# Attention and gated MLP on one core: q and k laid six tokens to a partition, later units cast by the Pool queue in order of use, tile 0 with gates ahead of values

## Chip, cores, metric

One of the cores of a Trainium2 chip runs the whole program. The metric is the device time of one execution in microseconds (us), the median of several runs. The span of a profile is some 1.7 us shorter than the time of the same execution, and moments within a run are counted from the span's start.

## The reference, cut to what matters

```python
def _attn_ref(q, k, v):                      # (8, 8, 576, 64) each, randn * 0.1
    scores = scale * np.matmul(q, k.transpose(0, 1, 3, 2))
    rel = pos[:, None] - pos[None, :]
    mask = (rel >= 0) & (rel < 64)           # causal, sliding window of 64
    scores = np.where(mask, scores, -1e9)
    attn = exp(scores - max); attn /= sum
    return attn @ v
def _moe_ref(x, w_gate, w_val, w_out):       # x: 4608 x 512, d_ff 1536
    return (np.maximum(x @ w_gate, 0) * (x @ w_val)) @ w_out
```

The inputs have a standard deviation of 0.1, so a score has one of about 0.01 (0.125 x 8 x 0.01) and the softmax is almost uniform in its window. A kernel that mixes up which token's q and k are which passes the comparison all the same.

## The kernel before

The sequence is worked in 24 units of 192 tokens (three per batch row); two units make a tile of 384 tokens. A unit's attention goes: load q and k, cast to FP16, transpose on VectorE (128x384 at a time), scores (`st`) on TensorE, exponential on ScalarE, values and row sums (`pv`) on TensorE, sums transposed, inverted and spread back on VectorE, and the normalised product (`xt`). A tile's MLP is 24 groups of four matmuls (`h`: 12 gate, 12 value groups) and 36 output matmuls (`op`). A small planner gives every step a wished time and so fixes the order of each engine's instructions; the engines then wait for data only.

```python
def qk_load(b, blocks=None, names="kq", two=False):      # a whole batch row (three units)
    ...
    eng = nc.gpsimd if b >= 2 else nc.scalar if two and g >= G // 2 else nc.sync
    eng.dma_start(nat[rows]...,                          # two tokens (512 B) to a run
        src[b, 2 * g:2 * g + 2].rearrange("h (m i j) d -> i (h m) (j d)", i=32, j=2))

def u_cast(u, name):                                     # rows 0 and 1 arrive as FP32
    if u < 3 and (u, name) not in ((0, "k"), (2, "k")):
        nc.scalar.copy(c16, src)
    else:
        nc.gpsimd.tensor_copy(c16, src)

def hidden(t, c0, c1, f0=0, f1=NF):                      # gate f, value f, gate f+1, ...
    for f in range(f0, f1):
        for i, wt in enumerate((wg, wv)):
            ...four matmuls into a bank of f_ps (4 banks)
...
    hidden(0, 0, U, 0, 4); ready(2); hidden(0, U, TT, 0, 4); hidden(0, 0, TT, 4)
    ready(3); hidden(1, 0, U)
    output_by_rows(0)
    ready(4); hidden(1, U, TT); output(1)
    for t in range(2, NU // 2):                          # the steady part
        ready(2 * t + 2); hidden(t, 0, TT); output(t)
```

"Second half of tile 0" below is `hidden(0, U, TT, ...)`: the first matmuls that need unit 1's `xt`. `heat` are matmuls on zeros that fill TensorE's idle time, meant to keep its clock up: the first four gate matmuls took 0.49 us in the changed kernel with eleven of them just before, and 0.80 without (e6).

The softmax here doesn't subtract the row's maximum and nothing guards it: scores larger than these inputs give would overflow.

## Time and profile before

| | us |
|---|---|
| time, median of 3 runs | 351.24 (350.97 to 351.8) |
| first gate matmul | 19.19 |
| second half of tile 0 starts | 25.65 |
| third tile (first of the steady part) starts | 82.48 (82.64 in the chain of waits, which the prediction uses) |
| each steady tile | 26.72 |
| tail | 27.16 |

Unit 1's `xt` is ready at 23.73, and the second half of tile 0 starts at 25.65 without a wait, behind the first half, which took 6.5 us:

```profile
7.13 3.44 POOL L192 DMA_DIRECT2D v<-in_v_dram  x4
...
22.77 0.96 DVE L343 TENSOR_TENSOR xt<-xv,rs 128x768 f16<-128x768 f32 x1 [0.37 <-ACT xv L318]
...
25.65 0.49 PE L398 MATMUL h<-xt,wg 128*128 128x192 f16 x4
```

### The profile page before, as it was taken

To read this page: it belongs to the slowest core of one execution; us is meant where nothing else is said; L and a number is where in the kernel's file an instruction comes from. 1 tells how busy PE (TensorE), PEld (TensorE's weight loads), DVE (VectorE), ACT (ScalarE), POOL (GpSimd) and SP (SyncE) were. 2 spreads that over 40 slices of the span, in tenths; PEclk is the share of its full clock that TensorE was granted. 3 is DMA by queue.
4 is the path that set the end of the run, shared out by engine and by line. 5 is a ranking of instruction groups with operands and counts; after the bars stand their busy time and mean duration, and the time that the engine had idled before them with its cause. 6 is when DMAs were issued, how large, how long until landed. Compare 5 with 4: busy or idle time off the path is not lost.

```text
span 350.3 us, 7421 instructions
## 1 busy us (share of the span) xinstructions
PE 334.8 (96%) x2910; PEld 200.6 (57%) x2910; DVE 232.9 (66%) x432; ACT 180.4 (52%) x346; POOL 89.2 (25%) x129
## 2 busy tenths in 40 slices
PE   8579989999999999999999999999999999999995
PEld 3467674865555655655665664664664664664652
DVE  6487756697766766766766766766776777675430
ACT  2745552746565464465564564563663663663331
POOL 5944022835110710134120720216110100000000
PEclk9859999999999999999999999999999999999999
DMA  6999999999833992429615894409906501001002
GB/s 189 165 204 191 213 196 95 186 94 189 91 25 99 90 97 92 32 18 184 81 11 112 63 111 107 30 3 158 121 2 104 49 2 60 33 0 62 30 2 90
DMA packets 95508, 32.21 MB, mean 92 GB/s; under 512 B 76017, under 2 KB 90865, under 8 KB 95473
## 3 DMA queue, kind: packets, MB, share of 16 engines
q0 software_dynamic: 80048, 17.57, 57.5%
q1 hardware_dynamic: 13760, 13.38, 13.3%
q10 hardware_dynamic: 1664, 0.79, 0.8%
q8 instruction: 23, 0.38, 0.4%
q14 instruction: 13, 0.10, 0.1%
HBM read 39.85 MB, written 9.44 MB: 141 GB/s over the span
## 4 chain that ended last, share of the span: by engine, by line
PE 70%; DMA 13%; DVE 8%; issue 4%; POOL 3%; SPq 1%; ACT 0%; DVEq 0%; POOLq 0%
PE h L398 37%; PE op L412 24%; PE pv L303 5%; DMA kn<-in_k_dram 5%; DVE g_sb L388 5%; DMA wv<-in_moe_w_val_dram 4%; DMA qn<-in_q_dram 4%; PE st L256 3%; DVE sT L329 3%; SPq L176 1%; POOL v L192 1%; DVE rT L335 1%; POOL wg L140 1%; POOL k L203 0%; POOL wv L140 0%
## 5 line engine op out<-in xcount | busy, mean ns | idle before, releaser
L398 PE MATMUL h<-xt,wv 128*128 128x384 f16 (+1 forms) x640 | 121.4, 313 | 2.7 <-DVE g_sb L388 1.4
L398 PE MATMUL h<-xt,wg 128*128 128x384 f16 (+1 forms) x640 | 121.3, 313 | 2.7 <-DVE xt L343 1.1
L388 DVE TENSOR_TENSOR g_sb<-r_sb,h 128x384 f16<-128x384 f32 (+1 forms) x160 | 79.6, 508 | 63.8 <-PE h L398 54.0
L385 ACT ACTIVATE r_sb<-h 128x384 f32<-128x384 f32 (+1 forms) x160 | 72.8, 464 | 57.9 <-PE h L398 43.3
L412 PE MATMUL op<-wo,g_sb 128*128 128x512 f16 x432 | 95.8, 379 | 0.5 <-DVE g_sb L388 0.3
L398 PEld LDWEIGHTS <-wg 128*128 128x128 f16 x640 | 60.7, 99 | 38.7 <-issue 4.7
L398 PEld LDWEIGHTS <-wv 128*128 128x128 f16 x640 | 60.5, 99 | 35.5 <-DMA wv<-in_moe_w_val_dram 2.1
L192 POOL DMA_DIRECT2D v<-in_v_dram x48 | 40.7, 851 | 156.4 <-PE pv L303 153.7
L412 PEld LDWEIGHTS <-g_sb 128*128 128x128 f16 x432 | 42.2, 98 | 49.9 <-issue 1.1
L329 DVE STREAM_TRANSPOSE sT<-pv 64x768 f32<-64x768 f32 x46 | 45.1, 980 | 23.4 <-ACT xv L318 20.3
L268 ACT ACTIVATE p<-st 128x512 f16<-128x512 f32 x96 | 53.0, 609 | 11.1 <-PE st L256 10.3
L419 ACT COPY o_sb<-op 128x512 f32<-128x512 f32 x36 | 20.9, 587 | 64.9 <-PE op L412 64.9
L318 ACT COPY xv<-pv 64x768 f32<-64x768 f32 x46 | 36.5, 793 | 25.9 <-PE pv L303 13.6
L272 DVE TENSOR_TENSOR p<-p,mask 128x512 f16<-128x512 f16 x88 | 33.7, 421 | 5.9 <-ACT p L268 5.7
L303 PE MATMUL pv<-p,v 128*128 128x128 f16 x368 | 25.4, 223 | 1.9 <-ACT p L268 1.9
L303 PEld LDWEIGHTS <-v 128*128 128x128 f16 x368 | 23.3, 100 | 5.1 <-DMA v<-in_v_dram 2.0
L337 DVE STREAM_TRANSPOSE rs<-rT 128x768 f32<-128x768 f32 x24 | 23.5, 978 | 0.8
L343 DVE TENSOR_TENSOR xt<-xv,rs 128x768 f16<-128x768 f32 x23 | 21.8, 949 | 0.8 <-ACT xv L318 0.4
L256 PE MATMUL st<-qT,kT 32*128 32x128 f16 x768 | 15.5, 215 | 1.6 <-DVE qT L216 1.2
L256 PEld LDWEIGHTS <-kT 32*128 32x128 f16 x768 | 11.3, 92 | 9.0 <-issue 7.6
L170 POOL DMA_DIRECT2D kh<-in_k_dram x24 | 15.8, 672 | 0.0
L170 POOL DMA_DIRECT2D qh<-in_q_dram x24 | 15.8, 679 | 0.0
(48 smaller groups left out, 80.7 us busy)
## 6 DMA issues: line engine op xcount, KB each, us to landing
out_dram<-o_sb SPq DMA_DIRECT2D x36, 256.0 KB, 2.0
v<-in_v_dram POOLq DMA_DIRECT2D x40, 128.0 KB, 4.1
kh<-in_k_dram POOLq DMA_DIRECT2D x24, 144.0 KB, 5.4
qh<-in_q_dram POOLq DMA_DIRECT2D x24, 144.0 KB, 7.1
wo<-in_moe_w_out_dram POOLq DMA_DIRECT2D x3, 512.0 KB, 15.9
kn<-in_k_dram SPq DMA_DIRECT2D x12, 96.0 KB, 7.1
qn<-in_q_dram SPq DMA_DIRECT2D x12, 96.0 KB, 5.9
wg<-in_moe_w_gate_dram POOLq DMA_DIRECT2D x2, 512.0 KB, 13.3
```

The costliest lines, as they stand in the source:

```text
L170: eng.dma_start(nat[rows].rearrange("p h m e -> p (h m) e"), src[b, 2 * g:2 * g + 2].rearrange("h (m i j) d -> i (h m) (j d)", i=32, j=2))
L192: nc.gpsimd.dma_start(v16[p0:128, w, :, 0:64], v[b, :, k0 + p0:k0 + 128].rearrange("h p d -> p h d"))
L256: nc.tensor.matmul(d["st"][g][:, (2 * hh + w) * 128:(2 * hh + w + 1) * 128], kT[rows, hh, ks + 128 * w:ks + 128 * w + 128, dh], d["qT"][ro ...
L268: nc.scalar.activation(d["p"][g].rearrange("p h c -> p (h c)"), d["st"][g], ACT.Exp, scale=scale)
L272: nc.vector.tensor_tensor(p, p, mask.rearrange("p w c -> p (w c)")[:, None, :].to_broadcast([128, 2, 256]), MUL)
L303: nc.tensor.matmul(pv[:, g, e, 64 * w:64 * w + 128], v16[:, w, c0:c0 + 128], d["p"][g][:, e, 128 * w:128 * w + 128], start=(e == 0 and w = ...
L318: nc.scalar.copy(d["xs"][rows], d["pv"][rows, :, g, 0:U])
L329: nc.vector.transpose(to[64 * e:64 * e + 64], d["pv"][64 - 64 * e:128 - 64 * e, :, e, 0:U])
L385: nc.scalar.activation(r_sb[:, 0:n], h1[:, 0:n], ACT.Relu)
L388: nc.vector.tensor_tensor(g_sb[:, f, c0:c1], r_sb[:, 0:n], h2[:, 0:n], MUL)
L398: nc.tensor.matmul(h[:, 0:n], wt[:, c, f * 128:f * 128 + 128], xt[:, c, c0:c1], start=(c == 0), stop=(c == NC - 1))
L412: nc.tensor.matmul(op, g_sb[:, f, bass.ds(sub * 128, 128)], wo[:, f], start=(f == 0), stop=(f == NF - 1))
```

## The change

Its intent: longer runs from memory (six tokens, 1,536 B), half the bytes landed for units 2 to 5 (the Pool queue casts on the way: 48 KB a transfer, where units 0 and 1 land 96), every transfer issued in the order in which it is used, gates before values in tile 0, and finer PSUM buffers for scores and values. Units 0 and 1 still arrive as FP32; VectorE now casts unit 1 and half of unit 0.

```diff
-    a_ps = ... tc.tile_pool(name="a_ps", bufs=1, space=PSUM)
+    a_ps = ... tc.tile_pool(name="a_ps", bufs=2, space=PSUM)      # two tiles of half the size
+    def qk_load(u, names="kq", queues=None):                       # one unit
+            for g in (0, 2, 1, 3):
+                part = src[b, 2 * g:2 * g + 2, U * uu:U * uu + U].rearrange("h (i j) d -> i h (j d)", j=6)
+                (nc.gpsimd if direct else queues[g // 2]).dma_start(nat[32 * g:32 * g + 32], part)
...
+            (nc.vector.tensor_copy if h or u else nc.scalar.copy)(c16[:, h], d[name][:, h])      # u_cast
...
-        nc.vector.transpose(dst.rearrange("p h (m i j) -> p h m j i", i=32, j=2), src)
+        nc.vector.transpose(dst.rearrange("p h (i j) -> p h j i", j=6), src)
...
+        for fb in range(f0, f1, each):                             # `each` gates, then `each` values
...
+        qk_load(0, "k", (nc.sync, nc.scalar))
+        qk_load(0, "q", (nc.sync, nc.scalar))
+        qk_load(1, "kq", (nc.sync, nc.sync))
...
+        W.at(3.0, lambda: v_load(0))
+        W.at(3.1, lambda: v_load(1))
+        ...six weight chunks at 3.2, q, k, v of unit 2, three w_out chunks, units 3, 4, 5
+        W.at(6.1, lambda: u_bias(1))
+        W.at(9.5, lambda: heat(11))
+        plan_unit(1, 9.0, (6.3, 7.5), (-1.8, -0.6), 1.3, None, 4.3, ...)
...
+        hidden(0, 0, U, 0, 4, 4); ready(2); hidden(0, U, TT, 0, 4, 4); hidden(0, 0, TT, 4, NF, 4)
+        output_by_rows(0)
+        ready(3); hidden(1, 0, U); ready(4); hidden(1, U, TT); output(1)
```

## The prediction

> **What bounds the kernel now.** I read the stretches first, because a busy share over the whole span mixes stages. Columns of this view: stretch, its length, then busy time and instructions of PE, PEld, DVE, ACT and POOL, granted clock, DMA share (it can pass 1[...]), GB/s.
>
> ```profile
> 0.00:19.19 19.19, 12.90 (x142) 7.11 (x143) 11.03 (x26) 8.67 (x15) 12.89 (x26) 0.90 1.16 180
> 19.19:40.00 20.81, 18.91 (x168) 13.66 (x169) 16.27 (x30) 11.51 (x24) 7.88 (x12) 0.85 1.43 200
> 40.00:62.00 22.00, 19.80 (x214) 13.86 (x216) 13.18 (x28) 9.49 (x23) 6.61 (x9) 1.00 1.25 153
> 62.00:82.64 20.64, 19.76 (x213) 14.06 (x208) 17.07 (x35) 11.84 (x27) 14.24 (x21) 1.00 1.60 150
> 82.64:109.37 26.73, 26.68 (x231) 15.47 (x229) 18.98 (x35) 14.52 (x27) 4.58 (x6) 1.00 0.78 97
> ```
>
> From 82.64 us on, each tile of 384 tokens takes 26.72 us and TensorE works 26.67 of it: nothing but fewer matmuls can help there. There are nine such tiles and a tail of 27.16 us. So the time is 82.64 + 9 x 26.72 + 27.16, and the change can win only before 82.64.
>
> Before it, the first gate matmul starts at 19.19. From there the work is two tiles, 31.5 of hidden matmuls (0.65 per group of four, 0.33 per half) and 15.5 of output, and units 2 to 5 at 1.57 each (0.57 scores, 0.89 values, 0.11 refill): 53.3 us. It takes 63.45: **10.1 us are lost**, and 19.19 us go before. The timeline of TensorE says where (start, duration, what, idle time and releaser):
>
> ```profile
> 19.19 0.80 PE L398 MATMUL h<-xt,wg 128*128 128x192 f16 x4 [1.08 <-DVE xt L343]
> 20.81 0.82 PE L398 MATMUL h<-xt,wv 128*128 128x192 f16 x4 [0.82 <-DMA wv<-in_moe_w_val_dram]
> ...
> 36.36 0.82 PE L398 MATMUL h<-xt,wv 128*128 128x384 f16 x4 [0.49 <-DMA wv<-in_moe_w_val_dram]
> ...
> 48.57 0.49 PE L398 MATMUL h<-xt,wv 128*128 128x192 f16 x4 [1.37 <-DVE g_sb L388]
> ```
>
> The first eight groups take 6.5 us where 2.6 would do: part waits, part half clock (0.50 granted from 20 to 25). The 1.37 at 48.57 is not VectorE's own slowness: its timeline has a transpose there that waited 1.62 for a Pool cast, and Pool had waited 4.77 for q. The chain of waits confirms it:
>
> ```profile
> 14.21 14.51 DMA wv<-in_moe_w_val_dram
> ...
> 33.68 6.73 DMA kn<-in_k_dram
> 40.42 5.73 DMA qn<-in_q_dram
> 46.17 7.17 DMA kn<-in_k_dram
> ...
> 53.84 5.63 DMA qn<-in_q_dram
> ```
>
> Apart from Pool's issuing, the path to 60 us is transfers, and the DMA view of 0 to 60 shows the engines full from 2.5 to 57 us with 10.97 MB moved. The head is **DMA-bound**.
>
> [...]weights (1,024 B landed per packet) run at about 205 GB/s between 20 and 26 us, a lone v load (128 B) lands 0.26 MB in 2.3 us, 113 GB/s. [...]q and k on SP and weights on Pool together keep near 200 GB/s, not twice that. [...]Output stores land in 2.0 us here.[...]
>
> **The change part by part.**
>
> *Layout.* Six tokens to a partition make runs of 1,536 B instead of 512 B. Units 2 to 5 are cast on the way instead of landing as FP32: 3.15 MB become 1.57 MB, 7 us of engine time in the head. Their Pool and ScalarE casts (0.83 each) go.
>
> *Pool's price.* Eight issues per unit instead of eight per three units. v issues of 512 and 1,024 runs took 0.69 and 0.88, so about 0.50 plus 0.37 ns per run; 64 runs should take 0.52. That is 4.2 us per unit against 1.8, and 6 with v, in a period of 13.3: hidden once steady. In the instruction order Pool keeps at most eight transfers in flight: each issue waits for the one eight before it. Small transfers therefore start late behind big weight chunks.
>
> *Order of use.* Previously unit 2's q and k (0.79 MB) went beside the first weights. Now the sum is: engines start at 1.75; q, k of units 0 and 1, 1.57 MB at 250 GB/s (the rate seen from 3 to 8 us), to 8.0; v0 and v1, 0.46 MB at about 130, 3.5, to 11.5; each 512 KB weight chunk 2.56 at 205. The first gate chunk lands near 14.1, the sixth near 26.9. Behind it the eight-in-flight rule lets q, k, v of unit 2 and then w_out issue only from 27 to 32; w_out moves from about 31 and its third chunk lands near **39.5**. The kernel's own plan says 38.1.
>
> *Matmul order.* Four gates ahead of four values fit a stream with gates first; tile 0's output now precedes tile 1. Tile 0's work, 23.4 plus unit 2's 1.57, fits between 14 and 39.5 and follows the weights, so it costs nothing. After the last w_out chunk come 12 output matmuls (2.6): 42.1. Tile 1 and units 3, 4, 5 are 15.9 + 7.8 + 4.7 = 28.4: **70.5** if TensorE never waits.
>
> *It will wait.* VectorE's work per unit: masks 4 x 0.38, k and q transposes 2 x 0.55, sum transposes 4 x 0.53 (estimated as half of the 0.98 of twice the size, plus overhead), 0.30 + 0.98 + 0.95 for the rest, 6.9 in all. While half of tile 1's hidden matmuls and one unit run, 9.5 us, VectorE has 12 products at 0.33 and about 6.7 of a unit: 10.6. Two halves put it some 2 us behind, and output cannot start without those products. Unit 5's q lands late too: w_out at 39.5, 17 q and k issues at 0.52, four v issues at 0.88, 2.5 to land: 54.4, where VectorE's order wants it near 52 to 53. That overlaps the backlog. I charge 2 us together: steady start **72.5**, a gain of 10.1.
>
> *Steady tiles.* Scores and values get two half tiles of PSUM. ScalarE copies go from 2 x 0.79 to 4 x 0.46 per unit (+0.27), the sum transposes from 2 x 0.98 to 4 x 0.53 (+0.16). Both engines have slack (19.0 and 14.5 of 26.7). The one stall per tile, about 0.2 us of TensorE waiting behind VectorE's long transposes, may shrink: 0 to 1.8 us, I take 1.0.
>
> Sum: 351.24 - 10.1 - 1.0 = **340.1**, rounded to 340.0.
>
> **Rivals.**
>
> *VectorE takes over.* If the sum transposes or the wider-strided k and q transposes (six elements apart instead of two) cost more than half-size pieces should, the overload between 42 and 72 grows. At 0.8 instead of 0.55 for each, a unit costs 1.5 more, two units in the critical stretch 3 us, and steady tiles would still hide it: 343. For it: 83% busy already from 62 to 82.64. Against: the same pass rate moves 128x384 in 0.54 to 0.58.
>
> *Pool's issuing and the eight in flight starve the engines.* If an issue costs 0.67 as the old ones did, unit 2 to 5's data slips by up to 4 us and the DMA view shows gaps from 27 to 32 and after 40. Then w_out lands at 41 and unit 5 stalls VectorE: 343 to 345. For it: Pool is already in the chain for 3% of the span; against: with its weights, units 0 and 1 need no Pool cast at all now.
>
> *Nothing lost.* If the order in the kernel is tuned to what the chip does, its plan puts the third tile's start at 69.05: a gain of 13.6, and with the stall gone 336.
>
> *Hidden anyway.* The head's transfers were not the bound and the path goes to the unchanged chain of unit 0 and 1 (cast, transpose, exp, normalise). That would leave 346 to 350. Against it: the chain of waits, and from 40 to 62 the loss comes from q and k landings that the change removes.
>
> **Range and chances.** 340.0, between 335.5 (nothing lost) and 345.0 (both congestion rivals in part). More than 2% faster means below 344.2, a gain of 7 out of an estimated 10 to 13; the lost time that I can point to and the DMA bytes saved agree on that size. Faster 0.87, within 2% 0.12, slower 0.01: nothing in the steady part gets more TensorE work.
>
> **What would show it.** Right: first gate matmuls at 12.5 to 14.5 with short waits for wg and wv until about 27; w_out landed by 38 to 41; the third tile starting at 70 to 74; tiles of 26.5 to 26.75 from there; no Pool cast left; kT and qT transposes still 0.54 to 0.58. Wrong: tiles above 26.9 (VectorE or Pool bound in the steady part), waits for k or q of over 2 us between 40 and 60, half clock after 20 us, or a first gate matmul later than 16.

The eight in flight are shown: before, Pool's tenth transfer (wv) landed at 28.72 and its eighteenth (wo) was issued at 29.00; in the changed kernel the tenth landed at 28.82 and the eighteenth was issued at 29.10. Estimates are the 7 us (1.57 MB at the 205 GB/s of weights would be 7.7), the 130 GB/s for v (113 for a lone load, 144 between 8 and 11.5 us together with k and q), the 2.5 us to land (the quickest q on SP's or ScalarE's queue took 2.4) and the halved copies and sum transposes (from 0.79 and 0.98).

## More of the kernel before

The head of the page, busy time and share of the span of each engine, then the busy tenths of the DMA engines in 40 equal slices:

```profile
PE 334.8 (96%) x2910; PEld 200.6 (57%) x2910; DVE 232.9 (66%) x432; ACT 180.4 (52%) x346; POOL 89.2 (25%) x129
DMA  6999999999833992429615894409906501001002
```

TensorE is busy 96% of the whole, and what it lacks lies in the first ten slices, where the DMA engines are full.

To see how q of unit 1, which will matter, arrives here, take VectorE's timeline (start, duration, instruction, idle time before it and who ended it):

```profile
10.10 0.58 DVE L216 STREAM_TRANSPOSE qT<-q 128x384 f32<-128x384 f32 x1 [1.31 <-ACT q L201]
10.83 0.58 DVE L216 STREAM_TRANSPOSE qT<-q 128x384 f32<-128x384 f32 x1 [0.15 <-ACT q L201]
```

Both units' q are transposed by 11.4 us. That q has landed by 9.24, when ScalarE casts it; Pool issues v only from 7.13 us on.

## The result

The changed kernel takes **349.45 us** (348.79 to 349.89, four runs) beside 351.3 us for the kernel before on the same chip. The ratio is 0.9945, with a 95% interval from 0.9924 to 0.9965. The change is 0.5% faster, "the same" at the 2% mark. The prediction of 340.0 (335.5 to 345.0) was too low by 9.4 us.

The page's head after, which answers the one shown of before:

```profile
PE 332.1 (96%) x2922; PEld 198.3 (57%) x2922; DVE 253.8 (73%) x485; ACT 185.2 (53%) x392; POOL 143.5 (41%) x245
DMA  9999999999728836828609728629519501001002
```

The stretches after, cut where the stages now begin (columns as in the prediction's first view):

```profile
0.00:20.24 20.24, 12.58 (x122) 5.60 (x123) 11.26 (x25) 7.63 (x16) 12.32 (x26) 0.83 1.25 186
20.24:48.76 28.52, 26.97 (x246) 17.22 (x245) 21.68 (x45) 11.45 (x29) 14.27 (x24) 1.00 1.12 152
48.76:71.97 23.21, 21.59 (x321) 19.08 (x320) 20.02 (x47) 16.02 (x43) 21.39 (x36) 1.00 1.11 133
71.97:81.67 9.70, 8.84 (x60) 4.43 (x53) 8.71 (x18) 5.61 (x11) 9.03 (x17) 1.00 1.24 143
81.67:108.20 26.53, 26.53 (x229) 15.48 (x229) 22.19 (x40) 14.62 (x30) 12.85 (x23) 1.00 0.66 80
```

The first gate matmul is at 20.24, a microsecond *later* than before and six later than forecast. The third tile starts at 81.67, not 72.5. The last tile starts at 320.26, so a steady tile takes (320.26 - 81.67) / 9 = 26.51 us, 0.21 less than before, and the nine of them give 1.9 us. The span shrank by 2.7 us: 0.8 of it before the third tile (82.48 to 81.67), 1.9 after. (The profiled run of before took 352.04 us, a little more than the three timed ones, so the spans differ by more than the medians.)

TensorE's timeline over the first 26 us:

```profile
15.29 1.04 PE L237 MATMUL st<-qT,kT 32*128 32x128 f16 x32 [3.21 <-DVE qT L197]
16.26 4.14 PE L215 MATMUL h<-zero 128*128 128x512 f16 x11
20.24 0.49 PE L388 MATMUL h<-xt,wg 128*128 128x192 f16 x4
...
25.03 1.48 PE L388 MATMUL h<-xt,wg 128*128 128x192 f16 x16 [0.63 <-DVE xt L331]
```

Unit 1's scores wait 3.21 us for its q. Then the fillers, at a granted clock of 0.58 (16 to 20.24 us), hold it to 20.2. Unit 1's values follow at 20.67, and its `xt` lets the second half of tile 0 start at 25.03. From there to 48.76, where tile 0's output ends, TensorE does not wait for a weight once. VectorE's timeline shows why unit 1 is late:

```profile
13.72 0.63 DVE L184 CAST qc<-qn 128x384 f16<-128x384 f32 x2 [2.33 <-DMA qn<-in_q_dram]
14.38 0.85 DVE L197 STREAM_TRANSPOSE qT<-qc 128x384 f32<-128x384 f32 x1
15.09 0.59 DVE L313 STREAM_TRANSPOSE sT<-pv 128x192 f32<-128x192 f32 x2
...
24.04 0.94 DVE L331 TENSOR_TENSOR xt<-xv,rs 128x768 f16<-128x768 f32 x1
```

q of unit 1 is there at 13.7 us, 2.3 us after the last q transpose of before had ended. Unit 0's sums (the third line) stand behind it in VectorE's order, so that both units of tile 0 wait for the one transfer. Unit 1's `xt` is ready at 24.98, 1.2 us *later* than before. The second half still starts 0.6 us earlier than before (25.65), because it no longer stands behind a first half of 6.5 us; that is all that the change bought at this point. The change itself brought v ahead of unit 1's q:

```profile
3.14 3.45 POOL L176 DMA_DIRECT2D v<-in_v_dram  x4
```

Pool now issues v from 3.14 us on, and SP the four transfers of that q from 5.36 to 7.09.

The chain of waits tells another story of the same stretch (start, duration, step):

```profile
3.95 7.06 DMA v<-in_v_dram
11.29 17.53 DMA wv<-in_moe_w_val_dram
...
32.86 11.18 DMA wo<-in_moe_w_out_dram
...
76.62 2.69 DMA q<-in_q_dram
80.00 0.84 DVE qT L197
```

It runs back through Pool's queue and would make the head a matter of transfers still. But its step to q of unit 6, landed at 79.31, is a near tie: VectorE's transpose of that q began at 80.00, right behind its own earlier work. The experiments have to decide between the two readings.

**Theory A**: unit 1's normalised half sets the start of the dense stretch, and everything after moves with it one for one. **Theory B** (what the prediction assumed): transfers and Pool's issuing set it. The expectations word A and B run by run; in e1, A still spoke of the first gate matmul.

### The profile page after: what moved, and what is told of

The parts are those of the page before. It is cut to its first block, busy times and chain, and to the rows that moved or that the text cites. A ratio compares the mean times of both kernels' runs of the same rounds, so it can differ in the third digit from the quotient of the medians. Undisturbed runs are those within 1.5% of the kernel's fastest.

```text
span 347.6 us, 7680 instructions
## 1 busy us (share of the span) xinstructions
PE 332.1 (96%) x2922; PEld 198.3 (57%) x2922; DVE 253.8 (73%) x485; ACT 185.2 (53%) x392; POOL 143.5 (41%) x245
## 4 chain that ended last, share of the span: by engine, by line
PE 75%; DMA 13%; POOL 8%; issue 2%; DVE 1%; ACT 0%; DVEq 0%; POOLq 0%
PE h L388 45%; PE op L402 22%; DMA wv<-in_moe_w_val_dram 5%; PE pv L288 5%; DMA v<-in_v_dram 4%; DMA wo<-in_moe_w_out_dram 3%; PE st L237 3%; POOL q L168 3%; POOL k L168 2%; POOL v L176 2%; DMA q<-in_q_dram 1%; POOL wo L145 0%; DVE qT L197 0%; DVE xt L331 0%; ACT o_sb L409 0%
## 5 line engine op out<-in xcount | busy, mean ns | idle before, releaser
L388 PE MATMUL h<-xt,wg 128*128 128x384 f16 (+1 forms) x640 | 118.2, 310 | 2.6 <-DVE xt L331 1.5
L388 PE MATMUL h<-xt,wv 128*128 128x384 f16 (+1 forms) x640 | 118.4, 310 | 0.6 <-ACT r_sb L373 0.5
L373 ACT ACTIVATE r_sb<-h 128x384 f32<-128x384 f32 (+1 forms) x160 | 74.1, 466 | 62.3 <-PE h L388 52.2
L402 PEld LDWEIGHTS <-g_sb 128*128 128x128 f16 x432 | 42.1, 98 | 49.3
L316 DVE STREAM_TRANSPOSE sT<-pv 64x384 f32<-64x384 f32 x88 | 51.1, 580 | 12.4 <-PE pv L288 11.1
L168 POOL DMA_DIRECT2D q<-in_q_dram x88 | 47.1, 552 | 22.5 <-DMA wo<-in_moe_w_out_dram 6.4
L253 DVE TENSOR_TENSOR p<-p,mask 128x512 f16<-128x512 f16 x88 | 34.3, 420 | 22.4 <-ACT p L249 22.3
L304 ACT COPY xv<-pv 64x384 f32<-64x384 f32 x88 | 41.6, 473 | 16.0 <-DVE sT L316 9.1
L168 POOL DMA_DIRECT2D k<-in_k_dram x88 | 47.4, 557 | 5.2 <-DMA wv<-in_moe_w_val_dram 2.0
L288 PE MATMUL pv<-p,v 128*128 128x128 f16 x352 | 23.6, 219 | 0.8 <-ACT p L249 0.5
L288 PEld LDWEIGHTS <-v 128*128 128x128 f16 x352 | 21.5, 98 | 4.0 <-issue 1.3
L197 DVE STREAM_TRANSPOSE kT<-k 128x384 f32<-128x384 f32 x22 | 18.8, 854 | 0.0
## 6 DMA issues: line engine op xcount, KB each, us to landing
wg<-in_moe_w_gate_dram POOLq DMA_DIRECT2D x3, 512.0 KB, 13.1
```

The source lines that it names most:

```text
L168: (nc.gpsimd if direct else queues[g // 2]).dma_start(nat[32 * g:32 * g + 32], part)
L253: nc.vector.tensor_tensor(p, p, mask.rearrange("p w c -> p (w c)")[:, None, :].to_broadcast([128, 2, 256]), MUL)
L288: nc.tensor.matmul(d["pv"][g // 2][:, g % 2, e, 64 * w:64 * w + 128], v16[:, w, c0:c0 + 128], d["p"][g][:, e, 128 * w:128 * w + 128], star ...
L304: nc.scalar.copy(d["xs"][rows, 2 * g:2 * g + 2], d["pv"][g][rows, :, e, 0:U])
L316: nc.vector.transpose(to[64 * e:64 * e + 64, 2 * half:2 * half + 2], d["pv"][half][64 - 64 * e:128 - 64 * e, :, e, 0:U])
L373: nc.scalar.activation(r_sb[:, 0:n], h1[:, 0:n], ACT.Relu)
```

## The experiments

The changed kernel's own marks are: second half of tile 0 at 25.03, third tile at 81.67, 56.64 us apart. The same three numbers for every experiment (from TensorE's timeline) are the most useful table. The marks come from one profiled execution each, and the runs were made on several chips, so times are compared by the ratio. The stretch "apart" is 56.64 or 56.65 in five runs that leave it alone and 56.40 or 56.41 in four with the shorter transposes, so 0.24 is more than its noise. The executions of e1, e5 and e9 fall into two groups 2 to 3 us apart; the profile of e5 is from the slower group, those of e1 and e9 from the faster.

| run | second half | third tile | apart | time, us | ratio to before (95%) |
|---|---|---|---|---|---|
| changed kernel | 25.03 | 81.67 | 56.64 | 349.45 | 0.9945 (0.9924 to 0.9965) |
| e1_order | 27.24 | 85.16 | 57.92 | 353.88 | 1.0061 (1.0022 to 1.0100) |
| e2_hw | - | 93.80 | - | 358.83 | 1.022 (1.018 to 1.026) |
| e3_merge | 24.94 | 81.58 | 56.64 | 349.73 | 0.9953 (0.9934 to 0.9972) |
| e4_stride2 (permuted) | 25.08 | 81.48 | 56.40 | 349.19 | 0.9929 (0.9913 to 0.9945) |
| e5_gate | 25.08 | 87.96 | 62.88 | 354.3 | 1.0064 (1.0014 to 1.0114) |
| e6_noheat | 26.16 | 82.81 | 56.65 | 350.57 | 0.996 (0.9937 to 0.9984) |
| e7_gate_noheat | 25.59 | 84.22 | 58.63 | 351.82 | 0.9999 (0.9974 to 1.0024) |
| e8_psum1 | 25.10 | 86.53 | 61.43 | 365.8 | 1.0402 (1.0364 to 1.044) |
| e9_vgate | 27.54 | 84.42 | 56.88 | 353.27 | 1.0065 (1.0016 to 1.0114) |
| e10_merge_stride2 (permuted) | 25.32 | 81.72 | 56.40 | 349.08 | 0.9929 (0.9912 to 0.9946) |
| e11_alt | 25.37 | 81.39 | 56.02 | 349.0 | 0.9926 (0.9908 to 0.9943) |
| e12_heat_early | 24.43 | 81.08 | 56.65 | 349.22 | 0.9937 (0.9913 to 0.9961) |
| e13_h6pv | 23.60 | 80.24 | 56.64 | 347.91 | 0.9902 (0.9881 to 0.9923) |
| e14_split | 23.48 | 80.58 | 57.10 | 348.12 | 0.9902 (0.9887 to 0.9916) |
| e15_h6pv_ms (permuted) | 22.99 | 79.40 | 56.41 | 347.55 | 0.9885 (0.987 to 0.9901) |
| e16_best (permuted) | 23.49 | 79.89 | 56.40 | 347.96 | 0.9906 (0.9889 to 0.9922) |
| e17_best_u3 (permuted) | 23.80 | 79.59 | 55.79 | 347.2 | 0.9875 (0.9858 to 0.9891) |
| e18_exact | 23.22 | 79.80 | 56.58 | 347.62 | 0.9909 (0.989 to 0.9929) |

### e1: unit 1 behind unit 0

```diff
-        plan_unit(1, 9.0, (6.3, 7.5), ...
+        plan_unit(1, 13.4, (10.4, 11.6), ...
```

> The changed kernel with unit 1 planned at 13.4 instead of 9.0, so that VectorE's program has unit 0's sums and TensorE's program the first gate matmuls ahead of what waits for unit 1's q. Theory A (the late q of unit 1, which sits ahead of unit 0's sums in VectorE's order, sets the first gate matmul at 20.24 us): the first gate matmul comes at 16 to 17.5, when the first weight chunk is there, tile 0's output ends 1.5 to 3 us before 48.8, and the time falls from 349.5 to 347 to 348. Rival B (the weights, whose last w_out chunk landed at 44.0, set the end of tile 0): the start moves, the end of tile 0 by no more than about 2 us, since 44.0 plus 2.6 is 46.6. Rival C (VectorE's load between 48 and 72 alone made the loss): the start moves and the time stays within 0.5 us.

The first gate matmul moved to 16.63 (after a wait of 2.11 for its weights), 3.6 us earlier. But the second half waited for unit 1 instead:

```profile
27.24 2.69 PE L388 MATMUL h<-xt,wg 128*128 128x192 f16 x16 [3.99 <-DVE xt L331]
```

The kernel got 4 us slower, which none of the three forecasts had. An early first matmul is worth nothing by itself; unit 1's end is what counts.

### e2: one transfer per head parity on the hardware queues

```diff
-            for g in (0, 2, 1, 3): ...dma_start(nat[32 * g:32 * g + 32], part)
+            for h in range(2): (nc.sync, nc.scalar)[h].dma_start(nat[:, h], ...all four head pairs)
```

> The changed kernel with q and k of units 0 and 1 brought by one transfer per head parity for all 128 partitions, eight transfers on SP and ScalarE instead of sixteen, so none of them waits for an earlier one to land. Theory A: unit 1's q lands by 9 to 10 instead of 13.7, VectorE is never held, the first gate matmul comes at 16 to 17 (the first weight chunk landed at 16.1), and the time is 346.5 to 348. If the q was late because v and the weights share the engines and not because it was issued late, it still lands after 12 and the start stays after 19. Rival C (VectorE's load later on): no change of the time.

In the changed kernel SP's issues of these loads had waited 0.8 and 0.2 us for earlier ones to land. But the run was confounded. The DMA engines' busy tenths in the first 30 us show it, the changed kernel's first, then this run's:

```profile
DMA  0049988999999999999999999999999999999973
```

```profile
DMA  0002124999999999999999999999998335645989
```

From 2 to 5 us the share is 0.1 to 0.2 for the most part, with a peak of 0.4, where the changed kernel's is 0.8 to 0.9, and unit 1's q landed at 25.9. So the transfers in their new shape left the engines mostly idle; how they were spread over the engines was not shown. The run says nothing of the number of issues.

### e3: two Pool transfers per tensor instead of four

```diff
+            if direct:
+                for h in range(2): nc.gpsimd.dma_start(nat[:, h], ...); continue
```

> The changed kernel with q and k of units 2 and later brought by two transfers of 128 runs per tensor instead of four of 64: half of Pool's issues. Theory B (Pool's issuing and the eight transfers in flight starve the engines between 28 and 32 us, so w_out lands at 44.0): w_out's third chunk lands at 41 to 42.5, Pool's busy time falls from 143 to about 100 us. By theory A this alone moves nothing before 48.8, since tile 0's matmuls did not wait for w_out: 348.5 to 350. If B sets the time: 346 to 347.5.

Pool then issues 44 transfers of k and 44 of q at 0.71 and 0.67 us each instead of 88 and 88 at 0.56 and 0.55. Pool is busy 111.3 us instead of 143.5. The third `w_out` chunk landed 1.4 us earlier (42.6 instead of 44.0), as Pool's issue behind it shows, first in the changed kernel, then here:

```profile
44.32 0.53 POOL L168 DMA_DIRECT2D q<-in_q_dram  x1 [2.04 <-DMA wo<-in_moe_w_out_dram]
```

```profile
42.85 0.70 POOL L169 DMA_DIRECT2D k<-in_k_dram  x1 [1.89 <-DMA wo<-in_moe_w_out_dram]
```

So the landing that theory B forecast (41 to 42.5) all but came about, and yet the third tile starts at 81.58, and the stretch is 56.64 us as in the changed kernel. Pool's issuing is not the bound. The chain of waits of this run no longer goes through Pool's queue. It goes through unit 1, from q over the fillers to `xt` and the second half:

```profile
6.77 7.21 DMA qn<-in_q_dram
...
16.86 3.45 PE h L220 x11
...
23.94 0.95 DVE xt L336
...
24.94 12.55 PE h L393 x92
```

### e4: transposes two tokens apart

```diff
-        nc.vector.transpose(dst.rearrange("p h (i j) -> p h j i", j=6), src)
+        nc.vector.transpose(dst.rearrange("p h (m i j) -> p h m j i", i=32, j=2), src)
```

The data still lie six tokens to a partition, so the transposed tokens are permuted: wrong, and within tolerance for the reason given with the reference.

> Wrong result on purpose: the q and k transposes write with the old pattern (two tokens apart, 8 bytes) over the same bytes, all else unchanged. Theory: the 0.85 us of these transposes against 0.55 before is their six-token spacing: they come back to 0.54 to 0.58. If VectorE's load between 48 and 72 us costs what the trace suggests, the third tile starts 1.5 to 3 us earlier and the time is 346.5 to 348. If it does not bind there: 349 to 349.5 with the transposes faster. A result of 0.85 still would mean that something other than the spacing slows them.

The groups by shape (instruction, count, busy time, mean ns of one, idle before it) for k, of the changed kernel, then of this run; q's are alike (846 and 540 ns):

```profile
L197 DVE STREAM_TRANSPOSE kT<-k 128x384 f32<-128x384 f32 x22 | 18.8, 854 | 0.0
```

```profile
L197 DVE STREAM_TRANSPOSE kT<-k 128x384 f32<-128x384 f32 x22 | 12.3, 559 | 0.8 <-DMA v<-in_v_dram 0.8
```

The wider spacing costs 0.3 us per transpose, and taking it away saves VectorE 13 us. Of that, 0.24 us reached the third tile. The prediction's rival had the size right (0.8 for 0.55) and the worth of it wrong.

### e5, e6, e7: weights held back; no fillers; both

```diff
+        W.at(3.15, lambda: nc.gpsimd.tensor_copy(gated, units[1]["q"][:, :, 0]) and None)   # e5, e7
-        W.at(9.5, lambda: heat(11))                                                         # e6, e7
```

In e5 a small Pool copy reads unit 1's q, and the weights are issued behind it.

> The changed kernel with one two-element Pool copy that reads unit 1's q ahead of the first weight transfer, so that weights are issued only when that q has landed. Theory A (unit 1's q lands at 13.7 because the weights, issued from 6.55 us, share the engines with it): it now lands at 9 to 10.5, unit 1's normalised half comes at 20 to 22 instead of 25.0, the first weight chunk still lands by 16 to 17. The end of tile 0 is then set by w_out (44 to 45, plus 2.6): 46.6 to 48, and the time 347 to 349. Rival (q is late because it is issued late, behind eight transfers in flight): it lands no more than 1.5 us earlier and the time is 349.5 to 351.

```profile
13.61 0.35 POOL L452 COPY gated<-qn 128x2 f32<-128x2 f32 x1 [7.03 <-DMA qn<-in_q_dram]
...
44.62 10.58 PE L402 MATMUL op<-wo,g_sb 128*128 128x512 f16 x36 [1.77 <-DMA wo<-in_moe_w_out_dram]
```

With no weight in flight, q of unit 1 still landed near 13.5: the weights do not delay it, contrary to this expectation's theory A. And weights issued 7 us later did not move the second half (25.08), which theory B cannot have. They only made w_out late, 20 us further on; so the weights had some slack, but less than 7 us. From the changed kernel's trace an estimate is 2.2: the third `w_out` chunk landed at 44.0, and the output that began at 40.99 reaches it after 24 matmuls of 0.216, at 46.2. The time, 354.3, lies above both forecasts.

> The changed kernel without the eleven idle-time matmuls ahead of tile 0, which stood at 16.26 to 20.24 us in TensorE's order between unit 1's scores and its values, 1.8 us beyond the exponentials that the values wait for. If they delay unit 1: its normalised half comes 1 to 1.8 us earlier than 25.0 and the time is 347.7 to 348.7. If what they save in clock is worth as much: 349 to 350, with the first gate matmuls at half clock.

Without fillers the first gate matmul came 0.8 us earlier (19.46), but the first four took 0.80 us instead of 0.49, and the second half 1.1 later; the third tile followed by 1.14. Even where they stand, the fillers are worth 1.1 us at these marks, more than either forecast had (349 to 350 at most, 350.57 measured).

> Both: weights held until unit 1's q has landed, and no idle-time matmuls. If the head is the path that A says, unit 1's normalised half comes at 19 to 21, and tile 0 waits for w_out: 346.5 to 348.5. If half clock at the start eats it: 348.5 to 350.

The second half came at 25.59 and w_out made the output wait 1.16. This one is a mix of the two and told nothing new; its time lies above both forecasts.

### e8: one PSUM tile for scores and values, as before

```diff
-            halves = [a_ps.tile([128, 2, 512], ...) for _ in range(2)]      # bufs=2
+            st = a_ps.tile([128, G, 512], ...)                              # bufs=1, likewise pv
```

> The changed kernel with scores and values in one tile of four banks with a single buffer, as before, and the halved copies and sums kept. If the halved PSUM tiles gave the steady gain (a tile takes 26.53 us against 26.72 before), tiles go back to about 26.7 and the time rises by 1.5 to 2, to 351. If the halved sum transposes gave it, tiles stay at 26.53 and the time within 0.5 of 349.5.

The steady tiles grew to (363.4 - 27.2 - 86.53) / 9 = 27.7 us (span 363.4). The plan of the changed kernel needs the halved tiles, since it takes sums earlier. The kernel before, with its own plan and one tile, needed 26.72; so the halves earn at most the 0.2 us that a tile gained and are a condition of the plan rather than its profit.

### e9: v of unit 1 and the weights held back

```diff
+        W.at(3.05, lambda: nc.gpsimd.tensor_copy(gated, units[1]["q"][:, :, 0]) and None)
         W.at(3.1, lambda: v_load(1))
```

> v of unit 1 and the weights wait on Pool until q of unit 1 has landed; only v of unit 0 goes ahead. If v of unit 1[...] is what delays q of unit 1, q lands at 10.5 to 11.5 us instead of 13.7, the transposed q follows within 1.6 us, and unit 1's xt is there near 22 to 23 instead of 25.0; the weights then start some 2 us later than in the changed kernel, so the time is 347.5 to 350. If late issue or v of unit 0 is the cause, q still lands at 13 or later, the weights are late as they were with the gate behind both v loads, and the time is 352.5 to 355.

q of unit 1 landed at 11.5, and VectorE did not wait for it:

```profile
11.48 0.63 DVE L184 CAST qc<-qn 128x384 f16<-128x384 f32 x2
```

Weights alone made no such difference (e5, 13.56), so v of unit 1 costs q 2.1 to 2.2 us. That is beyond the spread of 13.5 to 14.2 at which that q landed in runs with the changed kernel's loads. The queues in the first 14 us (packets, MB, share of 16 engines), e5 with both v and then e9 with v of unit 0 alone, neither with weights to speak of, stand beside it:

```profile
q0 software_dynamic: 3648, 0.46, 60.8%
q1 hardware_dynamic: 960, 1.18, 37.3%
```

```profile
q1 hardware_dynamic: 960, 1.18, 33.8%
q0 software_dynamic: 1685, 0.21, 23.8%
```

The packets of Pool's queue (q0), v in runs of 128 B (3,648 packets in e5), took 1.6 times the time of SP's (q1) for two fifths of the bytes. How the engines share their time between the two queues was not shown. The rest of q's delay (11.5 against the 8.0 of the prediction) is left to late issue and v of unit 0. Issue alone rules out 8.0: SP's last transfer of that q went out at 6.7 us, and no q transfer on SP's or ScalarE's queue landed in under 2.4 us in either kernel, which by estimate gives 9.1 at the earliest. The time got worse, as the weights now came late (first gate matmul waited 3.01 for them). The expectation had the landing right and the time wrong.

### e10: e3 and e4 together (permuted)

> Two Pool transfers per tensor instead of four, and the k and q transposes reading and writing two tokens apart (0.55 instead of 0.86 us); apart they gave 349.7 and 349.2. If the stage of tile 1 (32.9 us where 28.4 would do) is bound by VectorE's transposes and late Pool data jointly, the two together shorten it by 1 to 2.5 us: third tile at 79.2 to 80.7, time 346.5 to 348.3. If neither is on the path, the third tile starts at 81.3 to 81.7 as in each alone, time 348.8 to 349.8.

The stretch from second half to third tile shrank by 0.24, as with e4 alone. Neither Pool's issues nor the transposes, nor both, bind tile 1's stage. What little they gave is visible at its end. VectorE's timeline there, in the changed kernel:

```profile
79.32 0.82 DVE L197 STREAM_TRANSPOSE kT<-k 128x384 f32<-128x384 f32 x1
80.00 0.84 DVE L197 STREAM_TRANSPOSE qT<-q 128x384 f32<-128x384 f32 x1
80.68 0.94 DVE L331 TENSOR_TENSOR xt<-xv,rs 128x768 f16<-128x768 f32 x1
```

Unit 6's two transposes stand ahead of unit 5's `xt`, for which the third tile waits (0.87 us; 0.40 in e10).

### e11: gates and values alternate in tile 0 again

```diff
-        hidden(0, 0, U, 0, 4, 4); ... hidden(0, U, TT, 0, 4, 4) ... hidden(0, 0, TT, 4, NF, 4)
+        hidden(0, 0, U, 0, 4); ... hidden(0, U, TT, 0, 4) ... hidden(0, 0, TT, 4)
```

> Gates and values alternate again in tile 0, all else as changed. If gates ahead of values earn their keep only while weights arrive one behind the other, they are worth little here, since the first value weights (18.6 us) land before the first gate matmul (20.24) and the later ones before their use: dense TensorE from 25 on, time 349 to 350.3. The rival, that it is a main part of what was gained, gives waits on wv of 1 us and more in the first tile and 351 to 353.

Nothing was lost; if anything 0.3 us at the third tile was won. By 20 us the first two weight chunks are there (16.1 and 18.6), so gates ahead of values have nothing to hide. (The stretch is 0.6 us shorter, 56.02, with the same waits shown in tile 1, so that gain lies in tile 0.)

### e12, e13: the fillers into the wait, and unit 1's values first

```diff
-        W.at(6.1, lambda: u_bias(1))
-        W.at(9.5, lambda: heat(11))
+        W.at(8.9, lambda: heat(10, units[1]["st"][0]))      # e12; heat(6, ...) in e13
+        W.at(8.95, lambda: u_bias(1))
-        plan_unit(1, 9.0, (6.3, 7.5), (-1.8, -0.6), 1.3, None, 4.3, ...
+        plan_unit(1, 9.0, (6.3, 7.5), (-1.8, -0.6), 1.3, None, 3.4, ...     # e13 only: values before the first gates
```

> Ten filler matmuls go before unit 1's scores (into their banks, ahead of the bias) instead of eleven after them, so they fill the wait for the transposed q (12.1 to 15.3 us) and no longer stand in front of unit 1's values. If unit 1's completion sets the start of the dense stretch, the values move from 20.67 to 18 to 19, the second half of tile 0 from 25.03 to 23 to 23.5, out(0) ends at 47 and the time is 347 to 348.2. If the weights or the transfers set it, the second half waits on weights instead and the time stays at 349 to 350; if the clock drops for want of fillers in 16 to 20, the first matmuls run at half clock and half of the gain is lost.

Ten fillers were too many: they took 4.13 us (the eleven of e14 took 2.55) and ran to 16.2, so unit 1's scores came at 17.20 instead of 15.29. With none left between 16 and 20 the first four gate matmuls still took 0.49 us. The second half came 0.60 earlier and the third tile 0.59 earlier; the time (349.22) can't be told from 349.45. Mark and time fall short of what theory A forecast.

> Six filler matmuls ahead of unit 1's scores (in the wait for q), none after, and unit 1's values ahead of the first gate matmul in TensorE's order. If unit 1's second half is the only thing that sets the start of the dense stretch, it comes at 22.5 to 23.3 us instead of 25.03, and everything to the third tile moves with it, one for one: third tile at 79.2 to 80.0, time 347 to 348. If the weights or w_out take over, the second half starts early but waits of 1 us and more on weights appear (the second value chunk landed at 23.8, the third w_out at 44.0), and the time stays at 348.7 to 349.8.

```profile
18.02 0.30 PE L270 MATMUL pv<-p,v 128*64 128x128 f16 x4 [1.59 <-ACT p L249]
...
23.60 1.48 PE L388 MATMUL h<-xt,wg 128*128 128x192 f16 x16 [0.97 <-DVE xt L331]
...
80.24 0.81 PE L388 MATMUL h<-xt,wg 128*128 128x384 f16 x4 [0.88 <-DVE xt L331]
```

This settles it. No transfer was touched, and q of unit 1 even landed 0.5 us later than in the changed kernel (14.2). Unit 1's values came 2.65 us earlier, the second half 1.43 earlier, and the third tile 1.43 earlier. No wait on weights or w_out appeared, and the chain that ran through Pool's queue gave way by the same 1.43. **Theory A holds; theory B falls** as the bound of the changed kernel, though e14 shows `w_out` close behind. The second half and the third tile came 0.3 and 0.2 us after the forecast ranges, the time within its range. It is also an exact kernel, and faster than both (347.91).

### e14: unit 1's loads on two queues

```diff
-        qk_load(1, "kq", (nc.sync, nc.sync))
+        qk_load(1, "kq", (nc.sync, nc.scalar))
```

> k and q of unit 1 issued half on SP and half on ACT, all else as changed. If late issue on one queue (SP issued q at 5.4 to 7.1 us) is what makes unit 1's q late, q lands near 11.5 to 12.5 instead of 13.7, unit 1's half comes 1 us earlier or more and the time is 348 to 348.7, unless ScalarE's issuing makes unit 0 later by as much. If sharing with v is the cause, q lands at 13.2 to 14 as before, unit 0 is later by up to 1 us because ScalarE issues instead of loading its table, and the time is 349.2 to 350.5.

The time, 348.12, is what late issue would give, but for another reason. q was there only 0.8 us earlier (12.94, between the two forecasts), and unit 1's scores moved by 0.26 alone (15.03), since unit 0 became 2.6 us later while ScalarE was issuing (its table load began at 6.39 instead of 2.69).

```profile
15.92 2.55 PE L215 MATMUL h<-zero 128*128 128x512 f16 x11
...
44.99 2.75 PE L402 MATMUL op<-wo,g_sb 128*128 128x512 f16 x12 [0.21 <-DMA wo<-in_moe_w_out_dram]
```

Unit 0's later matmuls kept TensorE busy for 3.6 of the 4 us from 10 to 14, and the same eleven fillers took 2.55 us instead of 4.14 (at a granted clock of 0.58). That is the gain. How long a wait it takes to lose the clock, these runs do not say: in e9 the fillers took 3.81 us after waits of only 1.01 and 1.52. The last line shows the next limit: with the second half 1.5 us earlier, the last w_out chunk begins to be waited for.

### e15, e16, e17 (permuted), e18 (exact): do the remedies add up?

e15 is e13 with e3 and e4. e16 is e15 with five fillers, half of unit 1's q issued by ScalarE behind its table load, and unit 0's casts on VectorE alone. e17 is e16 with unit 3 planned earlier. e18 is e13 with e3 and the same earlier unit 3, every token in its place.

```diff
-        plan_unit(3, 41.0, (38.0, 40.0), ...
+        plan_unit(3, 38.5, (35.5, 37.5), ...      # e17, e18
```

> The order of e13 with two Pool transfers per tensor and transposes two tokens apart. If the stages add up, this gives the gain of e13 and the 0.3 to 0.4 us that the pair gave alone: third tile at 78.8 to 79.8, time 346.5 to 347.6, which would be the best of all. If the shorter transposes and issues stay off the path, it equals e13 within 0.3 us.

It did add up: 347.55, with the third tile at 79.40.

> e15 (fillers before the scores, five instead of six; merged Pool transfers; short transposes) with half of unit 1's q issued by ScalarE after its table load, and unit 0's casts all on VectorE. If issue order on the hardware queues is what was left, q of unit 1 lands 0.5 to 1 us earlier than in e15 without making unit 0 later, unit 1's half comes at 22.0 to 22.5 instead of 22.99, and the time is 346.5 to 347.3. If w_out takes over (e14 already showed a wait of 0.21 on its third chunk), the output rows of tile 0 wait on it by 0.5 us or more and the time equals e15's 347.55 within 0.3.

A miss. q of unit 1 landed 0.2 us earlier than in e15 (13.46, 13.62), not 0.5 to 1. v of unit 0 came later here (its matmuls waited to 10.96 us, in e13 to 10.02, in e15 to 10.38), the fillers stood behind them in TensorE's order, and unit 1's scores came at 16.34 although its q had been transposed by 14.75. No wait on w_out appeared.

> e16 with unit 3 planned 2.5 us earlier, so that its scores come among the last output matmuls of tile 0, where ScalarE and VectorE stand idle 3 to 5 us. If the stage of tile 1 is set by ScalarE and VectorE taking turns in the release of four PSUM banks, beside three units' work, it shortens by 0.7 to 1.5 us (from 32.7) and the time is 345.5 to 346.6. If something else sets it (late Pool data for units 4 and 5), it stays at 32.3 or more and the time is within 0.4 of e16's.

The stretch shrank by 0.6 us (56.40 to 55.79), a little under the forecast 0.7 to 1.5; the time, 347.2, met neither forecast. So part of tile 1's loss fits ScalarE and VectorE serving a third unit beside the release of the four PSUM banks; no run changes the number of banks, and most of the loss stays unexplained.

> e13 (347.91) with unit 3 planned 2.5 us earlier and two Pool transfers per tensor; tokens in their right places, unlike in e15 to e17. If the 0.6 us that moving unit 3 took from the stretch between the second half of tile 0 and the third tile (56.40 to 55.79, both with short transposes) is independent of the transposes, this kernel's stretch is 55.9 to 56.3 instead of 56.64 and its time 347.0 to 347.7. If the longer transposes (0.86) leave unit 3's q too late for the last output matmuls, TensorE waits there and the time is 347.8 to 348.3.

```profile
45.68 0.64 PE L242 MATMUL st<-qT,kT 32*128 32x128 f16 x32 [0.73 <-DVE qT L202]
```

With the longer transposes, unit 3's q was too late for its new place, by 0.73 us, and the stretch gained only 0.06. The time, 347.62, lies within the first forecast, but not for its reason. e13, e14 and e18 cannot be told from one another. All three compute the right thing and beat the changed kernel by about 0.4% (0.9902 to 0.9909 against 0.9945, each to the kernel before); for e13 and e14 the intervals are clear of the changed kernel's, for e18 they overlap a little.

## Why the prediction was wrong, point by point

**The step that failed is "Order of use", with the remark under "Matmul order" that tile 0's work "follows the weights, so it costs nothing".** It took TensorE's path from 14 to 42 us to be the weight stream. The stream itself came late: the chunks landed from 16.1 us on (14.1 was foreseen), 2.5 apart (2.56), and w_out's third at 44.0 where 39.5 was written. With the prediction's own 2.6 us behind it, tile 0 would have ended at 46.6. But unit 1 was ready later than all that. Tile 0 and unit 2 need 22.4 us of TensorE after the second half has begun (13.1 hidden, 7.8 output, 1.57). To end at the forecast 42.1, the second half had to start at 19.7. It started at 25.03, because q of unit 1 landed at 13.7 rather than by 8.0, unit 0's sums stood behind it, and fillers at a granted clock of 0.58 came next. That is **5.3 us** of the miss along the path taken. An earlier unit 1 alone would not have won them all: by the 46.6 above, w_out would have cost 4.5 of the 6.7 us between 42.1 and 48.76 in any case, and unit 1 stands 2.2 in front of it (an estimate; e14's wait of 0.21 on w_out, with the second half 1.5 earlier, points the same way). The prediction gave q and k 250 GB/s (its trace has 239 from 3 to 8 us) to themselves until 8.0 and v its turn after. In fact Pool issued v at 3.14 and v ran beside that q: v of unit 1 alone cost it 2.1 to 2.2 us (e9). Its fourth rival, "Hidden anyway", described just this chain and gave 346 to 350, where the time came out; it was dismissed on the evidence of a chain of waits that named transfers.

**The rest of the miss up to the third tile.** From 25.03 to 48.76 there are 1.3 us of small waits where none was foreseen. Tile 1's stage took 32.9 us where "It will wait" had 30.4 (28.4 and a charge of 2): **2.5 us**, the term that was mis-sized at 2 and measured 4.5. The sum, 5.3 + 1.3 + 2.5 = 9.1, accounts for the third tile at 81.67 instead of 72.5 (9.2). VectorE is busy 20.0 of 23.2 us there, so the direction was right. But it is not VectorE's total that binds: e4 and e10 took the transposes back to 0.55 us and gained 0.24. Moving a unit away gained 0.6 (e17). What holds the other 3.7 or so stays open; the timeline shows it as the 0.87 us at the third tile and many waits below 0.5 us in the turn from gate group to ScalarE to VectorE and back.

**Steady tiles.** Right in kind, a little better than reckoned: 1.9 us against 1.0. The stall per tile is gone (TensorE is busy 26.53 of 26.53).

**Costs of single operations.** Pool's issue of a q or k transfer: 0.52 foreseen, 0.55 measured. Sum transposes: 0.53 foreseen, 0.58 measured. ScalarE's copies: 0.46, and 0.47 measured. q and k transposes: 0.55 foreseen, 0.85 measured, and named as a rival. None of these moved the end by more than the 0.24 us of e4. By size, Pool's issue took 0.55 us for 64 runs, 0.67 to 0.71 for 128 (e3), and 0.86 on average for v (512 or 1,024 runs); Pool was busy 143.5 us of the span, nearly all of it issuing.

**The signs.** Of those listed as "wrong", one came true: a first gate matmul later than 16. Of those listed as "right", the tiles of 26.5 to 26.75 and the absence of Pool casts came true; the first gate matmul, w_out by 38 to 41, the third tile at 70 to 74 and the transposes at 0.54 to 0.58 did not. Two of these would have misled. e1 got the first gate matmul to 16.63 and was slower, and e4 got the transposes to 0.55 for nothing. The sign that mattered was not listed: what the second half of tile 0 waits for.

**Rivals.** "VectorE takes over" had the right size for the transposes and too much effect. "Pool's issuing and the eight in flight starve the engines" was right that gaps would appear (the DMA engines move 44 to 102 GB/s between 28.5 and 34.5 us) and w_out came later still than its 41 (44.0), but it was wrong that they bind (e3). "Nothing lost" fell with the rest.

## What to carry to other kernels

Before crediting saved bytes to the time, find the first instruction of the dense stretch and ask what it alone waits for; here a single 192-token half set everything that followed, one for one, until the next limit some 2 us behind it. Moving a transfer forward can push another back: v, issued 4 us earlier than before, made unit 1's q late (v of unit 1 alone by 2.1 to 2.2 us, e9). A chain of waits can run through a queue that is only almost as late as the true cause, so test it by moving the suspect and leaving the transfers alone. Fillers for the clock belong into a wait, ahead of what ends it, and no more of them than the wait is long: six there left the scores a wait of 0.59 us (e13), ten moved them from 15.29 to 17.20 (e12).
